# An S4D and SwiGLU layer on one core: an own DRAM tensor for the last spectra, other PSUM banks for the second FFN block, filler products, constant biases, and a new order table

## The chip, the cores and the metric

The kernel runs on one core of one Trainium2 chip. The metric is device time in microseconds (us) of one execution. Before the change three runs gave 954.37, 955.36 and 956.51, median 955.36. The trace is of one further, profiled execution of 954.89 us, whose span from the first to the last instruction is 953.1 us.

The engines are TensorE (PE: matrix products), VectorE (DVE), ScalarE (ACT), GpSimd (POOL) and SyncE (SP, which here only issues DMA transfers).

## The reference

Input `A_u` is 2048 positions of D = 640 channels in f32. A layer norm with modulation feeds an S4D convolution (a kernel of 2048 taps per channel, made from 128 complex modes, applied by FFT); its result, gated, is added. A second layer norm with modulation feeds a SwiGLU network with F = 1728, which is gated and added too.

```python
mod = (_silu(c) @ w_mod).reshape(c.shape[0], 6, 1, -1)
h = _layernorm(x) * (1 + ca) + sa
P = jnp.exp((A * dt[:, None])[:, :, None] * pos[None, None, :])
K = 2.0 * jnp.einsum("dn,dnl->dl", C, P).real
y = jnp.fft.irfft(jnp.fft.rfft(u_t, L2) * jnp.fft.rfft(K, L2)[None], L2)[:, :, :L]
x = x + ga * (y + h * D_skip)
h = _layernorm(x) * (1 + cb) + sb
x = x + gb * ((_silu(h @ w1) * (h @ w3)) @ w2)
```

## The kernel before, in words

**Convolution stage, 0 to about 355 us.** The 640 channels are five blocks of 128, each of eight chunks of 16 channels: 40 chunks, named by their first channel (`ph_0`, `ph_16`, ...). One chunk of the convolution's kernel is made by `gen_chunk`: POOL adds phases (`ph`) and multiplies magnitudes (`yy`, `xx`), ACT takes sines and cosines (`tr`), DVE multiplies them (`yy`, `xx`; the last multiplication is `xx<-tr,xx`), and PE forms the chunk's taps as 64 small products into `kps`, whose copy `ks` ACT takes away. The cosine is ACT's sine with a bias of half pi; that bias stands in a tile `hpi`. Around the chunks lie the modulation row (`pm`, `prow`, `rw`, `wb`), the first layer norm (ACT sums and squares `xs`, DVE statistics `h_st`, `h_mv`, a square root by Newton steps `rs_..._h`, normalised rows `hn`, `hb`) and the spectra: `ps`, `fh`, `fk` are products on the way to the frequency side, `fz` the last ones before the inverse, copied to `zt` and stored to DRAM as `zd`.

**Transition, about 355 to 430 us.** The inverse products `iy` read rows of `zd` back (`iz`, `xb`, `izb`). Channels 0 to 511 of the first eight row groups (two blocks of 512 positions, 0 and 1) come first (`iy0` to `iy7`); then the last 128 channels, whose spectra are made last, are stored and loaded back by `last_load` (tiles `izb0`, `izb1`, four transfers each, on SP's queue) for the products `iyb0` and `iyb1`. DVE adds them to the residual (`x`, `late`) and takes statistics (`st`, `mv`) and the Newton steps (`rs_..._n`); ACT and DVE normalise (`xn`); PE transposes (`tp`); ACT shifts (`v`) and splits into a high part (`x0h`, ...), DVE makes the low part (`x0l`, ...). The index in `x0`, `x1`, `x7`, `x4`, ... is only that of a buffer. The weights of the first FFN tiles are split likewise (`wh_u`, `wl_u`).

**FFN, about 376 us to the end.** The 1728 columns are 14 tiles (tile 13 is half), the positions four blocks of 512. Products with high and low parts (`hh`, `lh`, `hl`: three for one) give gate and up in `gu` banks. Tiles 0 and 13 come first for blocks 0 and 1: the steps `pp0.0` to `pp0.4` for block 0, `pp1.0` to `pp1.4` for block 1, each a fifth of the depth. The transposes `tp` of block 1 stand between them. Tile 1 follows as `pq0`, `pq1`, with the down products `dn0`, `dn13`, `dn1` between them, which add into five accumulator banks (`acc0` to `acc4`). From about 430 us on, groups of products for the other tiles and blocks run (`X`, `c`, `acc`); blocks 2 and 3 load their rows `iz8` to `iz15` by `inverse_row`.

**What sets the order.** Up to the first FFN group the kernel is a list of some 1690 tasks with what each needs. The text `ORDER` lists their numbers; `Plan.sequence` goes through it and checks that needs and buffers are met; `Plan.run` then issues each task, so each engine executes its tasks in this order and waits at a task whose inputs are not there. [...]

## Time and profile before

| stretch | what runs | us |
|---|---|---|
| profiled execution | one run | 954.89 |
| its span | first to last instruction | 953.1 |
| mean granted PE clock | whole span | 0.979 |
| PE busy | whole span | 870.5 |
| DVE busy | whole span | 682.3 |
| ACT busy | whole span | 551.5 |
| POOL busy | whole span, nearly all of it up to 320 us | 344.1 |

A row of the timeline gives the start, the duration, the engine, the line, the operation, output and inputs, the number of instructions that were joined in the row, and in brackets the idle time before it with what ended it. A granted clock of 1.00 is full speed of PE, 0.5 half. In the page's slices the busy share of the four computing engines and PE's clock, in tenths, lie like this over the span (40 slices of 23.8 us):

```profile
PE   1266999999989997899999999999999999999997
DVE  7988999999989878776676775657555555555412
ACT  3989999998877733644444444545444444443312
POOL 2698999999987400011111111000121212120000
PEclk9987999999999997999999999999999999999999
```

PE has little to do in the first four slices, while DVE, ACT and POOL are busy; slices 15 and 16 (357 to 405 us) are the transition.

### The profile page before, as it was taken

The page shows a single profiled execution, that of the slowest core. Times are in us where ns is not written, and L with a number is a line of the kernel's source. Part 1 is how long each engine was busy: PE and PEld are TensorE (multiplying, and loading weights), DVE is VectorE, ACT ScalarE, POOL GpSimd, SP SyncE. Part 2 cuts the span into 40 slices and gives each one's busy share as a digit, 9 for nine tenths or more (in the row PEclk, how much of TensorE's full clock was granted, in tenths as well). Part 3 has the DMA queues.
Part 4 walks back from the last instruction along what each step waited for, and adds up shares of the span by engine and source line. Part 5 has one row for each costly group of instructions (what it writes and reads, how often), then busy time and mean ns, then how long its engine had stood idle before and what let it go on. Part 6 is the DMA issues. An engine that isn't in the chain of part 4 may idle for free.

```text
span 953.1 us, 21244 instructions
## 1 busy us (share of the span) xinstructions
PE 870.5 (91%) x8369; PEld 689.6 (72%) x8369; DVE 682.3 (72%) x1290; ACT 551.5 (58%) x1036; POOL 344.1 (36%) x376
## 2 busy tenths in 40 slices
PE   1266999999989997899999999999999999999997
PEld 1134968877878875686777778888788888888775
DVE  7988999999989878776676775657555555555412
ACT  3989999998877733644444444545444444443312
POOL 2698999999987400011111111000121212120000
PEclk9987999999999997999999999999999999999999
DMA  9974454453173578754444412375432222221374
GB/s 199 284 266 112 158 134 137 101 146 83 47 173 93 134 189 212 179 179 125 148 116 123 139 63 91 92 237 168 130 91 84 83 84 83 84 84 38 110 217 132
DMA packets 110508, 127.42 MB, mean 134 GB/s; under 512 B 10568, under 2 KB 90696, under 8 KB 109128
## 3 DMA queue, kind: packets, MB, share of 16 engines
q1 hardware_dynamic: 110120, 125.80, 46.9%
q8 instruction: 66, 1.08, 0.5%
q14 instruction: 34, 0.28, 0.1%
q10 hardware_dynamic: 288, 0.26, 0.1%
HBM read 95.89 MB, written 30.15 MB: 132 GB/s over the span
## 4 chain that ended last, share of the span: by engine, by line
PE 55%; DMA 2%; ACT 2%; DVE 2%; SPq 1%; issue 1%; DVEq 0%
PE c L150 19%; PE acc L150 18%; PE X L150 12%; PE gu L150 3%; PE iy L150 1%; DMA w2r<-in_w 1%; DMA w<-w2d 1%; PE to L150 1%; PE tp L150 1%; PE gh L150 1%; ACT oc L978 0%; PE iyb L150 0%; SPq L991 0%; DMA izb<-zd 0%; DMA zd<-zt 0%
## 5 line engine op out<-in xcount | busy, mean ns | idle before, releaser
L150 PE MATMUL acc<-ah,w 128*128 128x512 f32 x560 | 173.0, 394 | 3.0 <-DMA w<-w2d 2.3
L150 PEld LDWEIGHTS acc<-ah,w 128*128 128x128 f32 x560 | 103.7, 188 | 26.6 <-issue 2.7
L775 POOL TENSOR_TENSOR s<-wr 128x256 f32<-128x256 f32 x22 | 16.6, 753 | 277.3 <-DMA wr<-in_w 133.0
L150 PE MATMUL acc<-al,w 128*128 128x512 f32 x260 | 102.2, 393 | 0.0
L599 DVE TENSOR_TENSOR wl<-s,wh 128x256 fp32r<-128x256 f32 x92 | 39.0, 424 | 67.3 <-ACT wh L598 66.8
L598 ACT ACTIVATE wh<-s 128x256 fp32r<-128x256 f32 x92 | 37.6, 410 | 78.3 <-PE X L150 57.9
L150 POOL TENSOR_TENSOR ph<-p,p 128x1024 int32<-128x1024 int32 x40 | 79.0, 1974 | 6.4 <-ACT tr L150 4.2
L598 ACT ACTIVATE wh<-wr 128x256 fp32r<-128x256 f32 x92 | 38.4, 418 | 57.6 <-PE X L150 42.0
L776 POOL TENSOR_TENSOR s<-s,wr 128x256 f32<-128x256 f32 x22 | 16.6, 753 | 132.2 <-issue 130.9
L150 DVE TENSOR_TENSOR yy<-yy,tr 128x512 f32<-128x512 f32 (+1 forms) x60 | 56.8, 947 | 6.3 <-POOL yy L150 3.3
L150 PE MATMUL kps<-yy,xx 128*32 128x64 f32 x1920 | 38.2, 230 | 22.4 <-DVE xx L150 19.9
L150 ACT ACTIVATE tr<-ph,hpi 128x512 f32<-128x512 f32 x80 | 54.4, 689 | 6.9 <-DVE yy L150 5.9
L836 ACT ACTIVATE t<-g 128x512 f32<-128x512 f32 x44 | 27.8, 632 | 52.7 <-DVE g L800 52.7
L150 PEld LDWEIGHTS acc<-al,w 128*128 128x128 f32 x260 | 48.9, 188 | 10.8 <-DVE al L599 0.4
L805 DVE SCALAR_TENSOR_TENSOR g<-t,g 128x512 f32<-128x512 f32 x48 | 33.7, 702 | 31.2 <-ACT t L836 29.3
L150 PEld LDWEIGHTS kps<-yy,xx 128*32 128x32 f32 x1920 | 32.7, 114 | 31.1 <-issue 17.5
L150 DVE TENSOR_TENSOR xx<-tr,xx 128x512 f32<-128x512 f32 x80 | 54.3, 683 | 0.7
L150 PE MATMUL fz<-fp,wz 64*128 64x512 f32 x224 | 54.5, 607 | 0.1
L599 DVE TENSOR_TENSOR wl<-wr,wh 128x256 fp32r<-128x256 f32 x92 | 40.7, 443 | 14.8 <-ACT wh L598 14.7
L150 ACT ACTIVATE tr<-ph 128x512 f32<-128x512 int32 x80 | 46.5, 598 | 4.2 <-DVE yy L150 2.7
L150 PE MATMUL ps<-wk,xb 128*64 128x128 f32 x640 | 46.8, 294 | 1.2 <-DVE hb L150 0.4
L598 ACT ACTIVATE ah<-h 128x512 fp32r<-128x512 f32 x26 | 16.5, 633 | 53.8 <-PE acc L150 53.8
(452 smaller groups left out, 2450.7 us busy)
## 6 DMA issues: line engine op xcount, KB each, us to landing
w<-w2d SPq DMA_DIRECT2D x42, 640.0 KB, 3.9
wr<-in_w SPq DMA_DIRECT2D x50, 320.0 KB, 3.6
zd<-zt SPq DMA_DIRECT2D x40, 256.0 KB, 2.5
w2d<-w SPq DMA_DIRECT2D x14, 640.0 KB, 3.5
xs<-in_x SPq DMA_DIRECT2D x16, 320.0 KB, 10.9
hs<-hb SPq DMA_DIRECT2D x20, 256.0 KB, 2.8
xb<-hs SPq DMA_DIRECT2D x20, 256.0 KB, 5.5
iz<-zd SPq DMA_DIRECT2D x32, 160.0 KB, 4.3
```

The source lines that it names most:

```text
L150: self.prev = self.k.order(f(*a, **kw), self.prev)
L598: self.nc.scalar.activation(H, v, AF.Copy)
L599: eng.tensor_tensor(Lo, v, H.bitcast(F32), op=ALU.subtract)
L775: eng.tensor_tensor(s[0], u[:, 0:2], u[:, 2:4], op=ALU.add)
L776: eng.tensor_tensor(s[1], s[0], g[:, 0:2], op=ALU.subtract)
L805: V.scalar_tensor_tensor(g, th, 1.0, g, op0=ALU.add, op1=ALU.mult)
L836: tanh = lambda o, i: A.activation(o, i, AF.Tanh, scale=0.5)
```

## The change

1. **`hpi` goes.** The bias of the cosines is the constant `HPI`.
2. **DRAM tensor `zl`.** The last block's spectra are stored there, `zd` keeps the other 512 channels. `last_load` reads block b's part with two transfers of 256 KB rather than four of 128 KB, one on SP's queue and one on ACT's. `inverse_row` needs eight transfers instead of four a row.
3. **Statistics.** The second layer norm takes a row's statistics in two instructions (512 and 128 columns) rather than five of 128; they are combined from 12 numbers instead of 30.
4. **Bank `small`.** One PSUM tile of 512 columns has the tag `kg` for good. `kps` is its columns 256 to 511; the first norm's sums, squares and statistics (`h_sum`, `h_ss`, `h_mv`) and two temporaries of the modulation are in its first columns.
5. **Fillers.** `wa0`, `wb0` to `wb4`, `wc0` and `wc1` are tasks of four 128x128 products of the identity with itself whose results nobody reads: `wa0` behind `iy7`, `wb0` before `iyb0`, the other `wb` between `iyb0` and `iyb1`, `wc` within `pq0`.
6. **Second block's first tiles.** `pp1` writes accumulator banks (`own=True`), so it takes no `gu` banks from `pp0`; `dn0`, which starts the accumulators, waits for `pp1`'s gates (`gm1.0`, `gm1.13`).
7. **`ORDER`** is a new list, and `Plan.sequence` counts buffers in use rather than asking for the oldest.

The core of the diff (the 1690 numbers of `ORDER` are left out):

```diff
+        self.small = psg.tile([P, 512], F32, name="small", tag="kg", bufs=1)
-                kps[c] = self.psg.tile([P, 256], F32, name=f"kps{b}{c}", tag="kg", bufs=1)
+                kps[c] = self.small[:, 256:]
-        for x in ("h_nm", "h_ss"):
-            setattr(self, x, self.gp.tile([P, NJ], F32, name=x))
+        self.h_nm = self.gp.tile([P, NJ], F32, name="h_nm")
+        self.h_sum, self.h_ss = self.small[:, 16:32], self.small[:, 32:48]
...
-                A.activation(t, ab[:, :, 4 - i, :], AF.Sin, scale=-SINS, bias=self.hpi)
+                A.activation(t, ab[:, :, 4 - i, :], AF.Sin, scale=-SINS, bias=HPI)
...
-        self.zd = d.tile([32, 2, 64, D], F32, name="zd")
+        self.zd = d.tile([32, 2, 64, D - P], F32, name="zd")
+        self.zl = d.tile([32, 2, 64, P], F32, name="zl")
...
-            for h in range(2):
-                for pr in range(2):
-                    t0 = 16 * (2 * pr + h) + 4 * b
-                    self.nc.sync.dma_start(z["b", b][h * 64:h * 64 + 64, pr], zv[:, t0:t0 + 4, cut:])
+            zl = self.zl.rearrange("f r (pr h t j) d -> (f r) h t pr (j d)", pr=2, h=2, t=4)
+            for h, e in enumerate((self.nc.sync, self.nc.scalar)):
+                e.dma_start(t[h * 64:h * 64 + 64].rearrange("p (r x) -> p r x", r=2), zl[:, h, b])
...
-                self.nc.sync.dma_start(z[pr][g * 64:(g + 1) * 64], zv[:, 16 * (2 * pr + g) + j])
+                for v, o in ((zv, slice(0, D - P)), (zl, slice(D - P, D))):
+                    self.nc.sync.dma_start(z[pr][g * 64:(g + 1) * 64, o], v[:, 16 * (2 * pr + g) + j, :o.stop - o.start])
...
-    def ln_part(self, st, xs, j, c0, c1):
-        for c in range(c0, c1):
-            self.nc.vector.bn_stats(st[:, j, c, :], xs[:, j, c * P:(c + 1) * P])
+    def ln_part(self, st, xs, j, c):
+        self.nc.vector.bn_stats(st[:, j, c, :], xs[:, j, 512 * c:min(512 * c + 512, D)])
...
+        def idle(n, place):
+            t = place()
+            for i in range(4):
+                nc.tensor.matmul(t[:, (i & 1) * P:(i & 1) * P + P], self.ident, self.ident, start=True, stop=True)
...
-                        banks[m] = [self.bank(f"gu{b}{m}{i}") for i in range(2 if m < 13 else 1)]
+                        banks[m] = [self.acc_bank(f"gu{b}{m}{i}", i if m < 13 else 2) if own else self.bank(f"gu{b}{m}{i}") for i in range(2 if m < 13 else 1)]
...
-        plain(1, (0, 13), "pp1.", 33, [])
+        plain(1, (0, 13), "pp1.", 33, [f"v1.{k}" for k in range(3)], True)
```

Three places show what the new order moves. The first is DVE's queue around chunk 0, whose last multiplication is the second `xx<-tr_0,xx`. Before:

```order
L150 SCALAR_TENSOR_TENSOR yy_315<-yy_315,tr_0_338 128x16x32
L150 BN_STATS h_st_235<-xs_230 128x6 x2
L150 COPY mag<-ptp 128x512
L150 BN_STATS h_st_235<-xs_230 128x6 x2
L150 TENSOR_TENSOR yy_315<-yy_315,tr_0_379 128x1024
L150 TENSOR_TENSOR xx_314<-tr_0_363,xx_314 128x512
L150 BN_STATS h_st_235<-xs_230 128x6 x2
L150 TENSOR_TENSOR xx_314<-tr_0_382,xx_314 128x512
```

In the changed kernel, on DVE around the same multiplication (`xx_272` is chunk 0, `xx_296` and `yy_297` chunk 1):

```order
L150 TENSOR_TENSOR xx_272<-tr_0_305,xx_272 128x512
L150 SCALAR_TENSOR_TENSOR small<-small,ct 128x5
L150 TENSOR_SCALAR sc<-small 128x5
L150 TENSOR_TENSOR xx_296<-tr_16_357,xx_296 128x512
L150 TENSOR_SCALAR h_nm<-small 128x4
L150 TENSOR_TENSOR xx_272<-tr_0_361,xx_272 128x512
L150 TENSOR_SCALAR pB<-ptp 128x4x128
L150 BN_STATS h_st_264<-xs_259 128x6 x2
L150 TENSOR_TENSOR yy_297<-yy_297,tr_16_338 128x16x32
L150 SCALAR_TENSOR_TENSOR yy_297<-yy_297,tr_16_338 128x16x32
```

The statistics `h_st` have moved behind chunk 0; before them stand small operations and one multiplication of chunk 1.

The second place is DVE's queue ahead of the add of `iyb0`, which starts the second norm of block 0. Before (the last rows of it):

```order
L150 TENSOR_TENSOR x_94<-iy_5338,x_94 128x512
L150 BN_STATS st_5020<-x_94 128x6 x2
L150 TENSOR_TENSOR late<-iy_5344,late 128x512
L150 BN_STATS st_5020<-x_94 128x6 x4
L150 TENSOR_TENSOR late<-iy_5357,late 128x512
L150 TENSOR_TENSOR late<-iy_5361,late 128x512
L150 BN_STATS st_5020<-x_94 128x6 x4
L150 TENSOR_TENSOR x_94<-iyb_5395,x_94 128x4x128
```

In the changed kernel, on DVE ahead of the same add (`st_4969` is block 1's, `st_4967` block 0's):

```order
L150 TENSOR_TENSOR late<-iy_5317,late 128x512
L150 TENSOR_TENSOR late<-iy_5321,late 128x512
L150 BN_STATS st_4969<-late 128x6
L150 TENSOR_TENSOR wl_u_5155<-wr_13_5041,wh_u_5154 128x128
L150 BN_STATS st_4969<-late 128x6
L150 TENSOR_TENSOR wl_u_5135<-wr_13_5041,wh_u_5134 128x256
L150 BN_STATS st_4967<-x_94 128x6 x2
L150 TENSOR_TENSOR x_94<-iyb_5362,x_94 128x4x128
```

Each statistics instruction now covers 512 columns, and two weight splits and block 1's statistics stand ahead of the add, which had come after it.

The third place is PE's queue at the second block's transposes and first products (`xn` are the normalised rows of block 1, `x4h`, `x4l` the first split operand of it, `gu_5679` and `gu_5618`, `gu_5620` the banks of `pp1`). Before, the end of the transposes and the start of `pp1`:

```order
L150 MATMUL tp_5664<-ident,xn_5623 128x128
L150 MATMUL tp_5664<-ident,xn_5606 128x128
L150 MATMUL tp_5664<-ident,xn_5604 128x128
L150 MATMUL tp_5664<-ident,xn_5617 128x128
L150 MATMUL gu_5679<-x4h_5669,wh_u_5065 128x512
L150 MATMUL gu_5679<-x4l_5670,wh_u_5065 128x512
```

In the changed kernel, on PE behind `pp1`'s first nine products:

```order
L150 MATMUL gu_5620<-x4h_5570,wl_u_5132 128x512
L150 MATMUL tp_5636<-ident,xn_5554 128x128
L150 MATMUL tp_5636<-ident,xn_5543 128x128
L150 MATMUL tp_5636<-ident,xn_5541 128x128
L150 MATMUL tp_5636<-ident,xn_5552 128x128
L150 MATMUL gu_5618<-x4h_5570,wh_u_5244 128x512
L150 MATMUL gu_5618<-x4l_5571,wh_u_5244 128x512
```

Before, all 20 transposes come first and `pp1` after them; now the transposes are put four by four between the steps of `pp0` and `pp1`, two of the five groups behind products of `pp1`.

More of the change, by code (lines that the diff above doesn't have):

```diff
@@ L228, in setup @@
         make_identity(nc, self.ident)
-        self.hpi = c.tile([P, 1], F32, name="hpi")
-        nc.gpsimd.memset(self.hpi, HPI)
         self.ones = c.tile([P, 1], F32, name="ones")
@@ L353, in h_stats @@
             st = self.gp.tile([P, 4, 2, 6], F32, name=f"h_st{b}", tag="h_st", bufs=1)
-            mv = self.gp.tile([P, 4, 2], F32, name=f"h_mv{b}", tag="h_mv", bufs=1)
+            mv = self.small[:, 64 + 8 * b:72 + 8 * b].rearrange("p (j a) -> p j a", a=2)
         def both(j):
@@ L1137, in tail_tasks @@
         ends = [f"z{b4}.{j}.o{f}" for j in range(4) for f in range(2)]
-        add("border", None, 0, border, ends + [f"ia{j}" for j in range(8)] + ["change"] + [f"wl0.{i}" for i in range(5)], 0)
+        add("border", None, 0, border, [f"wa{i}" for i in range(1)] + ends + [f"ia{j}" for j in range(8)] + ["change"] + [f"wl0.{i}" for i in range(5)], 0)
         def last_load(b):
@@ L1178, in mean @@
                 ln[b], steps[0] = self.ln_steps(self.fp, self.stats[b][1], f"n{b}")
-            add(f"lm{b}", "DVE", .68, mean, [f"isb{b}"] + [f"is{j}.{c}" for j in range(4 * b, 4 * b + 4) for c in range(2)], rank)
+            add(f"lm{b}", "DVE", .68, mean, [f"isb{b}"] + [f"is{j}" for j in range(4 * b, 4 * b + 4)], rank)
             if b == 0:
@@ L1230, in plain @@
                 need = [f"wl{m}.{i}" for m in tiles for i in ((k // 2,) if m == 13 else (4,) if k == 4 else (k // 2, 2 + k // 2))]
[L1231 removed]
+                add(p + f"{k}", "PE", .684 * len(take), lambda k=k: mm(k), [f"xl{b}.{k}"] + need + ([p + f"{k - 1}"] if k else after), rank, take=take if k == 0 and not own else [])
             last = [p + f"{KT - 1}"]
```

139 lines of the change are left out of this document (72 added, 67 removed), and 42 rows, old and new, of the table ORDER.

## The prediction

> **What bounds the kernel now.** The page names TensorE (PE) as the busiest engine, 91% of the span. Its idle rest is found with the view that cuts the span into stretches (columns: stretch, its length, PE busy, products, granted clock, DMA share, GB/s):
>
> ```profile
> core 0: us, PE busy (x), PEclk, DMA share, GB/s
> 0.00:50.70 50.70, 10.08 (x41) 0.95 0.94 251
> 50.70:80.00 29.30, 15.97 (x313) 0.79 0.59 192
> 80.00:100.00 20.00, 17.94 (x405) 0.91 0.67 169
> 100.00:355.00 255.00, 249.05 (x5044) 0.99 0.48 123
> 355.00:376.00 21.00, 15.40 (x83) 0.78 0.88 221
> 376.00:406.00 30.00, 26.45 (x116) 0.92 0.74 177
> 406.00:431.00 25.00, 23.84 (x105) 1.00 0.53 180
> 431.00:953.10 522.10, 511.74 (x2284) 1.00 0.38 115
> ```
>
> From 431 on PE works 511.74 of 522.1 us on instructions that the change leaves in order, so I cost that part at 0. From 100 to 355 it is busy 249.05 of 255, and F, the end of the last spectrum, lies where PE's work plus its idle time before puts it. That idle time is 100 − 10.08 − 15.97 − 17.94 = 56.0 us before 100, and 6 after. The view of waits up to 360 says for whom, and the timeline shows two of these waits:
>
> ```profile
> PE ptp L150 <- DVE wb L150: 25.1, 3, 9.4
> PE kps L150 <- DVE xx L150: 21.1, 6, 10.3
> ...
> 50.75 1.96 PE L150 MATMUL kps<-yy,xx 128*32 128x64 f32 x64 [7.65 <-DVE xx L150]
> 78.93 1.96 PE L150 MATMUL kps<-yy,xx 128*32 128x64 f32 x64 [10.35 <-DVE xx L150]
> ```
>
> So the early stage is worth what VectorE (DVE) brings forward for chunks 0 to 8. Behind F come the transition's waits, from the same view for 360 to 440:
>
> ```profile
> PE gu L150 <- ACT x4h L150: 2.1, 1, 2.1
> PE tp L150 <- ACT xn L150: 1.8, 1, 1.8
> PE iyb L150 <- DMA izb<-zd: 1.5, 2, 1.1
> PE c L150 <- DVE h L150: 1.2, 1, 1.2
> PE tp L150 <- DVE xn L150: 0.7, 1, 0.7
> PE gu L150 <- DVE x4l L150: 0.7, 1, 0.7
> ```
>
> **Term 1, the early order.** Ahead of chunk 0's last DVE product stand these two groups, as the view of groups by line and shape counts them (busy us, mean ns of one):
>
> ```profile
> L150 DVE BATCH_NORM_STATS2 h_st<-xs 128x6 f32<-128x320 f32 x8 | 3.5, 475 | 0.0
> ...
> L150 DVE COPY mag<-ptp 128x512 f32<-128x512 f32 x1 | 0.7, 670 | 0.0
> ```
>
> The new order puts all eight statistics and this copy behind it, 4.2 us. I add up every DVE instruction ahead of a chunk's last one in each program, at the durations of the rows before. The difference is −5.1 us at chunk 0, −8.4 at 1, −4.5 at 2, −3.9 at 3, between −1.8 and −5.2 at 4 to 9, −7.8 at 39, the last. For POOL it is +0.9, −4.5, +0.3, +2.6, +6.5 and +5.5 at chunks 0 to 5 and between −2 and +4.3 from 6 on. ACT gains through the constant:
>
> ```profile
> L150 ACT ACTIVATE tr<-ph,hpi 128x512 f32<-128x512 f32 x80 | 54.4, 689 | 6.9 <-DVE yy L150 5.9 <-DVE xx L150 0.3
> ...
> L150 ACT ACTIVATE tr<-ph 128x512 f32<-128x512 int32 x80 | 46.5, 598 | 4.2 <-DVE yy L150 2.7 <-POOL ph L150 0.7 <-DVE xx L150 0.5
> ```
>
> The 80 cosines read a bias from SBUF and take 689 ns, the 80 sines without it 598. If the bias is the reason, 80 × 0.091 = 7.3 us go from ACT; its moved work adds 3.4 up to the last chunk. Neither is on the path directly, since PE is the bound from 100 on.
>
> PE's own work to its last chunk is the same in both, so F moves by the idle time before 100, and that by the lead with which chunks 6 to 8, the last before PE is dense, come: −2.2 to −3.2. I take **−3**. The ends: −7, near the last chunk's lead, if each lead is kept; +3, if the bank described under the second rival eats the lead.
>
> **Term 2, the last spectra's way through DRAM and the first normalisation.** F is the end of the first row of the timeline here; behind it stand three groups:
>
> ```profile
> 350.04 4.67 PE L150 MATMUL fz<-fp,wz 64*128 64x512 f32 x16
> ...
> 358.99 5.21 SPq L150 DMA_DIRECT2D izb<-zd  x8
> ...
> 365.23 0.69 DVE L150 TENSOR_TENSOR x<-iyb,x 128x512 f32<-128x512 f32 x1 [1.00 <-PE iyb L150]
> ...
> 371.91 4.53 PE L150 MATMUL tp<-ident,xn 128*128 128x128 f32 x20 [1.80 <-ACT xn L150]
> ...
> 387.88 2.40 PE L150 MATMUL tp<-ident,xn 128*128 128x128 f32 x20 [0.74 <-DVE xn L150]
> ...
> L150 DVE BATCH_NORM_STATS2 st<-late 128x6 f32<-128x128 f32 x20 | 4.3, 279 | 0.0
> ...
> L150 DVE BATCH_NORM_AGGREGATE mv<-st 128x2 f32<-128x30 f32 x8 | 1.4, 245 | 0.0
> ...
> L150 DVE BATCH_NORM_AGGREGATE h_mv<-h_st 128x2 f32<-128x12 f32 x4 | 0.4, 160 | 0.0
> ```
>
> F = 354.71. Eight load issues, 0.65 us each, make SyncE send izb1's last at 364.2; four on two queues end 1.3 us after they begin, so block 0's landing comes about 1 us and block 1's about 3 us earlier. That doesn't bring the add of 365.23 forward: DVE now stands ahead of it. Between the last zt copy (end 0.74 after F, 355.45) and that add it has 8 adds of about 0.66 (5.3), 7 statistics of 512 columns and two weight splits (0.7). No row shows 512 columns; back to back one of 128 takes 4.3/20 = 0.22 and one of 320 3.5/8 = 0.44, and a straight line gives 0.65, so 4.55 in all; the bounds are 0.44 and 0.86, four of 128. The add starts at 366.0, **+0.8** (by the bounds −0.7 to +2.3). Four aggregates of 12 numbers instead of 30 give 4 × (1.4/8 − 0.4/4) = 0.3 back. tp starts **0.5 later** against F.
>
> Fillers: wb1 to wb4 are 16 products of 0.12 (2.40/20), 1.9 us, in a wait of PE's, so they cost 0. They end with iyb1 near 366.5, and some 5.5 us of idle PE remain until tp at 372.4. The stretch 355 to 376 has a mean clock of 0.78 and the 20 tp products there took 4.53, against 2.40 in the second block. I take tp at half clock again, 0; the other end is 4.53 − 2.40, −2.1.
>
> [...]
>
> **Term 3, first to third FFN tile.** One stretch, from the first gu product to the first X, and rows inside it:
>
> ```profile
> 376.09:428.27 52.18, 48.63 (x212) 0.96 0.66 181
> ...
> 386.35 0.91 ACT L150 ACTIVATE xn<-late,rs_n_n,rs_y_n 128x640 f32<-128x640 f32 x1
> ...
> 390.92 0.78 ACT L150 ACTIVATE v<-tp,cols 128x512 f32<-128x512 f32 x1
> ...
> 399.50 0.62 ACT L150 ACTIVATE x8h<-v 128x512 fp32r<-128x512 f32 x1
> ...
> 403.32 0.39 PE L150 MATMUL gu<-x8h,wh_u 128*128 128x512 f32 x1
> ...
> 405.15 0.39 PE L150 MATMUL gu<-x8h,wl_u 128*128 128x512 f32 x1
> ```
>
> It lasts 52.2 us. By the order it holds 190 products and tp1's 20 (two more reach over its edges). At (405.15 − 403.32)/8 = 0.229 and with tp1's 2.40 they make 45.9; 6.3 is waits and half clock. Now tp1 lies between pp0's and pp1's steps, pp1 has its own banks, and block 1's ACT normalisation isn't queued behind a weight copy (the 386.35 row, now some 4 us earlier). So the waits on xn and x4h (0.7 + 2.1 + 0.7) go and the half clock behind them with it. What comes: wc0 and wc1, 8 × 0.12 = 1.0; the start at half clock, 0.6; and a wait that is late next, on x5 and x8 of block 1, which stand behind gate work and tile 1's weight splits on ACT and DVE. In the old order ACT took 9 us from the first v (390.92) to x8h's end, a little more than pp0's and pp1's steps that now cover it, so I bound this wait by 0 and 5 and take 2.2, near the old one of 2.1 + 0.7. Sum: −6.3 + 1.0 + 0.6 + 2.2 = **−2.5**. With +0.5 the transition is −2.0 (from −5 to +1). The 1.2 us on DVE h I leave.
>
> **No cost.** Row loads iz8 to iz15 take 64 issues instead of 32, on SyncE, early against PE in a part where DMA is 0.38 busy; uncovered, 4 more issues of 0.65 a row delay an inverse row by 2.6 us, which PE passes by other products. The rsqrt's extra temporary costs 0.
>
> Sum against the profiled execution, 954.89: −3 − 2 = 949.9. It lies 0.47 below the median of the three runs, so the forecast for the median is **950.4**.
>
> **Rivals.**
> *Only the transition gains* (chance 0.15): POOL, with +2.1 to +6.5 of work ahead at chunks 3 to 7, and not DVE, releases the chunks; F stays: 953.4. For it speaks that POOL, too, has little idle time there; against it, that the waits name DVE xx.
> *Slower through the shared bank* (0.15): chunk products, ACT's sums and squares and DVE's aggregates now write the one bank `small`. In the new program chunk 0's product waits for a square, the next square for that product's end, chunk 1's product for an eviction queued behind another square, and DVE's aggregate for chunk 1's product.
>
> ```profile
> L150 ACT ACTIVATE ks<-kps 128x256 f32<-128x256 f32 x40 | 15.0, 375 | 4.9 <-PE kps L150 4.7
> L150 ACT ACTIVATE xs<-xs,h_nm 128x640 f32<-128x640 f32 x12 | 9.8, 813 | 0.5 <-DVE h_nm L150 0.5
> ```
>
> One round is a cold product (1.96, the 50.75 row), a square (0.81) and an eviction (0.38), 3.2 us; three rounds are at most 10. It decides once more than chunk 3's lead of 3.9 is lost. Half of the excess of 6 is F + 3; with 1 us less of the transition's gain, since ACT then also enters it later, 957.
>
> [...]
>
> *All is kept* (0.17): leads of 6 us in F, and no late x5, x8: −6 − 5 = 944.
> *The fillers and the pair of queues do nothing* (0.08): tp is cold in any case, DVE sets the add, and x5 and x8 eat term 3: 952.4.
>
> **Numbers.** Forecast (947 to 953 at the median) 0.45; the four rivals 0.15, 0.15, 0.17, 0.08. A difference within 0.2%, 1.9 us, can't be told from none. The first rival lies at that border, half of it counts as same; with a share of the forecast's upper edge: faster 0.72, same 0.13, slower 0.15. The range leaves out the outer halves of the extremes: 943.5 to 957.
>
> **What would show it.** Right: first kps product near 46, chunk 3's near 75, F near 351.7; cosine rows near 600 ns; the iyb0 add about 11.3 us after F, ended by DVE's queue and not by izb; tp still 4.5 us; gu to X in 49.7 us. Wrong: PE waiting on ACT squares or DVE aggregates before 70, F later than 355, or a wait of over 4 us on x5, x8 or weights of tile 1.

## The result: 979.3 us after, 955.0 before

Four runs of the changed kernel have a median of 979.34 us (976.82 to 981.41), four of the kernel before beside them 954.95 (954.37 to 956.51). The ratio is 1.0252, with a 95% interval of 1.0223 to 1.0280: the change makes the kernel slower by 24 us. The forecast was 950.4, in a range of 943.5 to 957.

The profiled execution of the changed kernel took 978.61 us, its span is 976.8 (953.1 before). Split at the prediction's marks (F is the end of the last spectrum, X the first product into a bank `X`, with which the third FFN tile begins), the 23.7 us by which the span grew lie for the most part in two of three parts, ahead of F and behind X:

| | before | after | difference |
|---|---|---|---|
| start to F | 354.71 | 367.56 | +12.85 |
| F to first transpose tp | 17.20 | 16.57 | −0.63 |
| F to first gu product | 21.38 | 19.46 | −1.92 |
| F to X | 73.56 | 75.74 | +2.18 |
| X to the end (the tail) | 524.83 | 533.50 | +8.67 |

### The profile page after: what moved, and what is told of

Its sections match the earlier page's. It is cut to its first block, busy times and chain, and to the rows that moved or that the text cites. A ratio compares the mean times of both kernels' runs of the same rounds, so it can differ in the third digit from the quotient of the medians.

```text
span 976.8 us, 21320 instructions
## 1 busy us (share of the span) xinstructions
PE 885.8 (91%) x8433; PEld 694.7 (71%) x8433; DVE 675.0 (69%) x1235; ACT 549.4 (56%) x1043; POOL 350.1 (36%) x375
## 4 chain that ended last, share of the span: by engine, by line
PE 72%; DVE 10%; ACT 7%; issue 3%; DMA 2%; SPq 1%; DVEq 0%; ACTq 0%
PE c L150 19%; PE acc L150 17%; PE X L150 12%; PE ps L150 6%; PE small L150 4%; PE fz L150 4%; PE fh L150 3%; PE fk L150 3%; DVE fp L150 1%; PE iy L150 1%; PE gu L150 1%; DMA w2r<-in_w 1%; DVE yy L150 1%; DVE xx L150 1%; ACT tr L150 1%
## 5 line engine op out<-in xcount | busy, mean ns | idle before, releaser
L150 PE MATMUL acc<-ah,w 128*128 128x512 f32 x560 | 175.3, 398 | 1.7 <-DMA w<-w2d 1.2
L150 ACT ACTIVATE tr<-ph 128x512 f32<-128x512 f32 (+1 forms) x160 | 93.6, 600 | 7.9 <-DVE yy L150 4.0
L775 POOL TENSOR_TENSOR s<-wr 128x256 f32<-128x256 f32 x22 | 17.4, 791 | 176.6 <-DVE wl L597 86.5
L150 PE MATMUL ps<-wk,ks 128*64 128x128 f32 x640 | 42.9, 286 | 14.6 <-DVE hb L150 8.6
L777 POOL TENSOR_TENSOR s<-wr 128x256 f32<-128x256 f32 x22 | 18.8, 853 | 96.9 <-ACT wh L150 65.2
L150 PEld LDWEIGHTS ps<-wk,ks 128*64 128x64 f32 x640 | 37.1, 143 | 20.4 <-issue 12.9
```

Of the source, the lines that this page charges most:

```text
L150: self.prev = self.k.order(f(*a, **kw), self.prev)
L775: eng.tensor_tensor(s[0], u[:, 0:2], u[:, 2:4], op=ALU.add)
L777: eng.tensor_tensor(s[2], g[:, 0:2], u[:, 0:2], op=ALU.subtract)
```

## The profile after

The view of stretches, cut at the same events (stretch, its length, PE busy, products, granted clock, DMA share, GB/s):

```profile
core 0: us, PE busy (x), PEclk, DMA share, GB/s
0.00:50.70 50.70, 9.28 (x53) 1.00 0.92 227
50.70:80.00 29.30, 16.10 (x272) 0.78 0.53 153
80.00:100.00 20.00, 16.02 (x330) 0.84 0.86 227
100.00:367.60 267.60, 252.99 (x5148) 0.99 0.47 123
367.60:387.00 19.40, 18.23 (x132) 1.00 0.91 212
387.00:418.00 31.00, 26.01 (x120) 1.00 0.62 178
418.00:443.30 25.30, 25.30 (x111) 0.93 0.36 102
443.30:976.80 533.50, 521.87 (x2291) 1.00 0.38 116
```

Three things are to be seen. Between 100 and F PE was idle for 6 us before; now it is for 267.60 − 252.99 = 14.6. Behind F the clock is 1.00 where it was 0.78. And in the last row PE is as busy as before, at full clock, but busy for 521.87 us where the tail before had 513.3: the same products take longer.

Of PE's waits on `DVE xx` in the first 100 us, 20.5 us before, the view of waits has 1.3 left; others have taken their place, and PE is idle for 58.6 us before 100 where it was 56.0:

```profile
PE ptp L150 <- DVE wb L150: 30.6, 3, 15.1
PE ps L150 <- DVE hb L150: 8.6, 1, 8.6
```

The timeline of all engines between 50 and 67, cut to the bank `small`, shows the round of rival two:

```profile
50.21 1.95 PE L150 MATMUL small<-yy,xx 128*32 128x64 f32 x64
...
52.58 0.83 ACT L150 ACTIVATE xs<-xs,h_nm 128x640 f32<-128x640 f32 x1 [1.99 <-PE small L150]
55.32 0.39 ACT L150 ACTIVATE ks<-small 128x256 f32<-128x256 f32 x1
...
57.70 0.83 ACT L150 ACTIVATE xs<-xs,h_nm 128x640 f32<-128x640 f32 x1 [1.50 <-PE small L150]
62.17 0.97 DVE L150 BATCH_NORM_AGGREGATE small<-h_st 128x2 f32<-128x12 f32 x4 [3.79 <-ACT xs L150]
...
63.64 0.83 ACT L150 ACTIVATE xs<-xs,h_nm 128x640 f32<-128x640 f32 x1 [1.02 <-DVE small L150]
```

ACT's squares wait for chunk products, DVE's aggregate waits for ACT's squares, the next square for the aggregate: 8.3 us of such waits in 12 us (1.99, 1.50, 3.79 and 1.02), of operations that share no number and only a bank. Whether operations that share a bank need such waits, no run here shows. They are waits of ACT and DVE, not of PE; what they cost F, the experiments show.

The cosines, in the view of groups by line and shape (busy us, mean ns of one):

```profile
L150 ACT ACTIVATE tr<-ph 128x512 f32<-128x512 f32 x80 | 47.1, 599 | 4.6 <-DVE xx L150 2.1 <-DVE yy L150 1.6
```

They take 599 ns instead of 689, as forecast. DVE's timeline behind F, cut to the last statistics ahead of the add of `iyb0`:

```profile
377.38 1.28 DVE L150 BATCH_NORM_STATS2 st<-x 128x6 f32<-128x512 f32 x2
378.58 0.67 DVE L150 TENSOR_TENSOR x<-iyb,x 128x512 f32<-128x512 f32 x1
```

The add starts 11.0 us after F and waits for nothing but the instructions ahead of it. The transition on PE, first the second norm and then the places with fillers and waits:

```profile
374.51 1.16 PE L150 MATMUL small<-ident 128*128 128x128 f32 x8
375.73 1.16 PE L150 MATMUL wb<-ident 128*128 128x128 f32 x8
...
377.84 4.81 PE L150 MATMUL wb<-ident 128*128 128x128 f32 x32
...
384.13 0.33 PE L150 MATMUL tp<-ident,xn 128*128 128x128 f32 x1 [0.46 <-ACT xn L150]
384.94 2.29 PE L150 MATMUL tp<-ident,xn 128*128 128x128 f32 x19 [0.48 <-ACT xn L150]
...
408.75 0.50 PE L150 MATMUL gu<-x5l,wh_u 128*128 128x512 f32 x1 [1.06 <-DVE x5l L150]
411.39 0.50 PE L150 MATMUL gu<-x8l,wh_u 128*128 128x512 f32 x1 [0.23 <-DVE x8l L150]
417.93 1.52 PE L150 MATMUL wc<-ident 128*128 128x128 f32 x8 [3.01 <-DVE h L150]
424.67 1.05 PE L150 MATMUL wc<-ident 128*128 128x128 f32 x8
...
447.02 0.50 PE L150 MATMUL c<-x1h,wh 128*128 128x512 f32 x1 [2.16 <-DVE h L150]
```

A filler task of four products shows as eight in the records and takes 1.16 to 1.2 us ahead of tp. With these fillers the clock is 1.00 from 367.6 to 387.0 (no_wb, below, is the kernel without them), and the transposes take 2.6 us; before, they took 4.53 us, at a granted clock of 0.50 from 371.9 to 376.1. `wc0` waits 3.01 us, since the accumulator bank that it writes still holds `pp1`'s gates.

## The experiments

Where the table gives no interval, one run was made, and a single run says little about 3 us: eight runs of one kernel below lie between 949.75 and 958.47. F and the other marks come from one profile of each kernel, F as the end of its last `fz` row, and repeat better. Five kernels share the changed kernel's program up to F but for addresses or fillers, and their F lies between 366.8 and 369.6; three share that of the kernel before but for addresses (before, before_st512, before_wp0), and theirs lies between 354.3 and 355.6.

| kernel | time, us | ratio to before (95%) | F | chunk 30 | F to X | tail | spacing |
|---|---|---|---|---|---|---|---|
| before | 954.95 | | 354.71 | 266.3 | 73.56 | 524.83 | 0.2291 |
| after | 979.34 | 1.0252 [1.0223, 1.0280] | 367.56 | 278.5 | 75.74 | 533.50 | 0.2333 |
| st_old | 971.96 | 1.0155 [1.0102, 1.0208] | 368.06 | 279.6 | 75.39 | 528.25 | 0.2291 |
| before_st512 | 964.67 | 1.0094 [1.0055, 1.0133] | 355.58 | 267.2 | 75.29 | 532.73 | 0.2333 |
| pad24 | 968.74 | | 366.76 | 277.6 | 75.14 | 525.10 | 0.2273 |
| before_wp0 | 965.17 | 1.0115 [1.0033, 1.0196] | 354.32 | 265.9 | 77.08 | 532.90 | 0.2333 |
| order_old | 970.19 | 1.0137 [1.0099, 1.0175] | 356.99 | 268.8 | 78.66 | 532.85 | 0.2333 |
| small_split | 977.63 | 1.0214 [1.0174, 1.0254] | 363.00 | 274.4 | 75.70 | 536.60 | 0.2333 |
| old_split | 968.08 | | 352.81 | 265.6 | 80.87 | 532.62 | 0.2333 |
| before_hpi | 954.53 | 0.9990 [0.9955, 1.0026] | 351.69 | 266.2 | 74.91 | 527.00 | 0.2291 |
| mid_split | 976.76 | | 358.97 | 273.5 | 77.32 | 538.71 | 0.2333 |
| strict | 1015.81 | 1.0622 [1.0572, 1.0673] | 404.60 | 316.0 | 76.87 | 535.33 | 0.2333 |
| strict_split | 1014.02 | | 399.66 | 311.0 | 76.98 | 535.56 | 0.2333 |
| bank_split | 976.05 | | 362.02 | 275.7 | 76.88 | 535.30 | 0.2333 |
| knot30 | 978.88 | 1.0240 [1.0184, 1.0295] | 366.54 | 270.5 | 75.73 | 535.63 | 0.2333 |
| no_wc | 977.42 | | 369.58 | 280.4 | 69.66 | 536.36 | 0.2333 |
| no_wb | 982.37 | | 368.06 | 278.2 | 76.09 | 536.45 | 0.2333 |
| best1 | 956.94 | | 352.83 | 265.9 | 71.15 | 531.22 | 0.2291 |
| best3 | 998.15 | 1.0433 [1.0383, 1.0484] | 398.37 | 309.7 | 69.33 | 530.20 | 0.2292 |

Chunk 30 is the start of the small product that closes it. Spacing is the mean distance, in us, from the start of one 512-column product to the start of the next in the tail, over the some 2,000 pairs of each trace that start 0.21 to 0.25 us apart.

### The tail: where the FFN's weights lie

The first theory on the tail was an address: the third part of the change makes the tile `ln_st` smaller, and the FFN's tiles behind it move. By the allocations in the built programs, the activations of the FFN's products then start at 32 modulo 128 bytes of a partition instead of 96, and their weights at 96 instead of 32. st_old gives the tile its old size back and uses a part of it:

```diff
-        return (pool.tile([P, 4, 2, 6], F32, name=f"st_{tag}", tag="ln_st", bufs=2),
+        return (pool.tile([P, 4, KT, 6], F32, name=f"st_{tag}", tag="ln_st", bufs=2)[:, :, :2, :],
```

> The changed kernel with the statistics tile of the second norm kept at its old size of 480 bytes (only 192 are used), so that every FFN operand lies at the SBUF address, modulo 128, that it had before the change (moving operand 96, weights 32; in the changed kernel 32 and 96). Address theory: the 512-column products of the FFN return from one every 0.2333 us to one every 0.2287, some 2200 of them, so the time falls by about 10 us to 969; the conv stage stays as it is (last spectrum's end near 367.6). Rival theory, the slower spacing comes from something else in the changed program (the order of the PSUM banks, other transfers beside it): the spacing stays 0.233 and the time 979.

before_st512 does the opposite to the kernel before, and nothing else:

```diff
-        return (pool.tile([P, 4, KT, 6], F32, name=f"st_{tag}", tag="ln_st", bufs=2),
+        return (pool.tile([P, 4 * KT * 6 + 8], F32, name=f"st_{tag}", tag="ln_st", bufs=2)[:, :4 * KT * 6].rearrange("p (j c s) -> p j c s", j=4, c=KT),
```

> The kernel before with the statistics tile made 32 bytes larger, nothing else: FFN operands get the addresses modulo 128 of the changed kernel (32 and 96). Address theory: the spacing of FFN products rises from 0.2287 to 0.2333 us and the time from 955 to about 965. Rival theory, something else in the changed program: 955 and 0.2287.

Both move the spacing by the whole difference. The row of 800 to 900 in the view of stretches, where PE has almost no wait, shows it as products in 100 us, before and after:

```profile
800.00:900.00 100.00, 99.62 (x441) 1.00 0.23 73
```

```profile
800.00:900.00 100.00, 100.00 (x430) 1.00 0.24 73
```

There are 438 products in that row of st_old and 429 in that of before_st512, and the clock is 1.00 in all four. Eight floats of padding in the kernel before cost 8.1 us (964.67 against 956.57 beside it), the old tile size gives the changed kernel 7.4 back (979.34 to 971.96). Which operand's address matters, two paddings tell. In pad24 a constant tile of 40 floats becomes one of 24, so that of the two operands only the weights move, to 32; in before_wp0 a tile of 32 becomes 24, and the weights move to 0:

```diff
-        c.tile([P, 40], F32, name="pad")
+        c.tile([P, 24], F32, name="pad")
```

> The changed kernel with the constants' pad 64 bytes shorter: the FFN weights' addresses go from 96 back to 32 modulo 128, the moving operands stay at 32 (96 before). If the weights' address is what slows the products, the spacing returns to 0.229 us and the time to about 970; if it is the moving operands' address, the spacing stays at 0.233 and the time near 979.

> The kernel before with the constants' pad 32 bytes shorter: the FFN weights' address goes from 32 to 0 modulo 128, nothing else. With the weights at 32 the 512-column products come every 0.229 us, at 96 every 0.233. If the cost is that a weight row of 512 bytes begins late in a line of 128, 0 is as good as 32 or better: 0.229 or less, time 955 or up to 10 us less. If only 32 is good, 0 is slow too: 0.233 and 964.

| kernel | activations, mod 128 | weights, mod 128 | products from 800 to 900 | spacing, us |
|---|---|---|---|---|
| before | 96 | 32 | 441 | 0.2291 |
| st_old | 96 | 32 | 438 | 0.2291 |
| pad24 | 32 | 32 | 443 | 0.2273 |
| after | 32 | 96 | 430 | 0.2333 |
| before_st512 | 32 | 96 | 429 | 0.2333 |
| before_wp0 | 96 | 0 | 429 | 0.2333 |

In these six traces the weights' address decides between two groups: at 32 the products follow each other in 0.2273 to 0.2291 us, at 0 and 96 in 0.2333, with the activations at 96 as at 32. With the weights at 32, pad24 is a little faster still (0.2273 against 0.2291); whether that is its activations' address or another tile that moved with the padding, one kernel can't tell. 64 was not tried. The first theory for before_wp0, that the late start of a weight row costs the time, fails, since 0 is as slow as 96; why 32 is the fast one, no run here shows. The 0.0042 us on the tail's 2,106 products of 512 columns are 8.8 us, and PE's busy time in the tail went from 513.30 to 521.87, 8.57 more; so the tail's 8.67 are explained by it. Beside that, tails of one spacing differ from profile to profile, from 524.83 to 531.22 us at the fast one and from 532.62 to 538.71 at the slow one, and no run shows why.

### Up to F: bank and order

order_old is the changed kernel with the old order, task by task (new tasks beside their neighbours):

```diff
-ORDER = """(the new list)"""
+ORDER = """(the old list's order, in the new tasks' numbers)"""
```

> The changed kernel with the old order table, carried over task by task (the fillers put at the places that the new order gives them, a row's statistics where their second part stood). Order theory: the late end of the last spectrum comes from the new order; it returns from 367.6 to about 355 and the time falls by some 10 us to 967 to 970. Bank theory: the waits on the one PSUM bank for first-norm sums, squares and chunk products make the loss; then they appear in this order too (PE or ACT waiting on each other between 45 and 70 us), the last spectrum ends at 362 or later and the time stays above 972. Address theory is not touched: product spacing 0.2333.

small_split keeps the new order and puts sums, squares and statistics back into SBUF tiles; old_split does both:

```diff
-        self.h_sum, self.h_ss = self.small[:, 16:32], self.small[:, 32:48]
+        self.h_sum, self.h_ss = (self.gp.tile([P, NJ], F32, name=x) for x in ("h_sum", "h_ss"))
...
-        th, u = self.small[:, :KT], self.small[:, 8:8 + KT]
+        th, u = (e.tile([P, KT], F32, name=x) for x in ("th", "thu"))
...
-            mv = self.small[:, 64 + 8 * b:72 + 8 * b].rearrange("p (j a) -> p j a", a=2)
+            mv = self.gp.tile([P, 4, 2], F32, name=f"h_mv{b}", tag="h_mv", bufs=1)
```

> The changed kernel with the first norm's sums, squares, statistics and the modulation's temporaries back in SBUF tiles, so that only chunk products use the bank. Bank theory: ACT's waits of 2.0 and 1.5 us on PE, DVE's of 3.8 us on ACT and PE's on DVE between 50 and 66 us go, chunk 3 comes 3 to 5 us earlier, and the last spectrum's end falls from 367.6 by as much; the time is 972 to 976. Order theory: the waits go, but chunks 4 to 39 are held by the order, and the time stays within 2 us of 979. Product spacing stays 0.2333 in both.

> The changed kernel with both: the old order table, and the first norm's sums, squares and statistics in SBUF tiles. It closes a square of four: with the new order the last spectrum ends at 367.6 (shared bank) and 360.6 (SBUF tiles), with the old order at 357.0 (shared bank). If order and bank were independent, the two would add up and this kernel would end its last spectrum near 350.0. If the bank costs what the waits in the old order show, some 2 us, and the new order's 5.9 us are its own, it ends near 354.7, that of the kernel before, and the time is about 968.

F in the four kernels: 367.56 (new order, bank), 363.00 (new, SBUF), 356.99 (old, bank), 352.81 (old, SBUF). For small_split that is the end of its last `fz` row:

```profile
358.34 4.66 PE L150 MATMUL fz<-fp,wz 64*128 64x512 f32 x16
```

The expectations that name small_split's F give 360.6, a time at which these products still run, and what they work out from it is 2.4 us off. With 363.0 the sum of the two parts, had they nothing to do with each other, would be 352.4 for old_split, and 352.81 was measured: they add up. The bank costs 4.2 us of F with the old order and 4.6 with the new, and the order costs 10.2 us without the bank and 10.6 with it. The chunks (start of the product that closes each, and F) show where each loss comes in:

| chunk | before | old order, SBUF | new order, SBUF | new order, bank (after) |
|---|---|---|---|---|
| 1 | 62.0 | 62.0 | 58.3 | 57.3 |
| 3 | 80.8 | 80.8 | 79.4 | 83.9 |
| 6 | 99.1 | 98.9 | 97.7 | 102.0 |
| 7 | 105.0 | 104.4 | 107.1 | 111.4 |
| 29 | 261.2 | 260.4 | 261.4 | 265.6 |
| 30 | 266.3 | 265.6 | 274.4 | 278.5 |
| 39 | 328.9 | 327.1 | 336.1 | 340.7 |
| F | 354.71 | 352.81 | 363.00 | 367.56 |

The bank's loss is there by chunk 3 and passes unchanged to F, 4.1 to 4.6 us at each row of the table from chunk 3 on. It lies where the waits between 50 and 66 are. In the time it can't be told from noise: 979.34 and 977.63 have intervals that overlap, and of order_old and old_split (970.19 and 968.08) the second ran once. The order's cost is clear in the time too (979.34 against 970.19). What remains, 352.81 against 354.71, can be the constant, which before_hpi tries alone in the kernel before:

```diff
-                A.activation(t, ab[:, :, 4 - i, :], AF.Sin, scale=-SINS, bias=self.hpi)
+                A.activation(t, ab[:, :, 4 - i, :], AF.Sin, scale=-SINS, bias=HPI)
```

> The kernel before with the constant as the bias of the cosines, nothing else (the tile stays, so that no address moves). ACT's 80 cosines take 600 ns instead of 689, 7 us less ACT work in the conv stage. The old order with SBUF tiles and the other parts of the change ended its last spectrum 1.9 us earlier than the kernel before; if the constant is the cause, this one does too and the time is 953.5. If PE alone sets that end, no change: 955.4.

F falls by 3.0 there, and the time can't be told from none (0.9990, 0.9955 to 1.0026).

Where does the order lose its 10 us? The rows of old_split in the view of stretches, and those of small_split, with only the order between them:

```profile
0.00:100.00 100.00, 42.89 (x751) 0.95 0.80 223
100.00:250.00 150.00, 146.20 (x3038) 1.00 0.43 112
250.00:300.00 50.00, 47.58 (x1042) 1.00 0.43 105
300.00:352.80 52.80, 52.24 (x968) 1.00 0.66 163
```

```profile
0.00:100.00 100.00, 44.68 (x755) 0.95 0.77 206
100.00:250.00 150.00, 144.17 (x3032) 1.00 0.45 120
250.00:300.00 50.00, 42.27 (x884) 0.97 0.39 93
300.00:363.00 63.00, 61.20 (x1130) 1.00 0.62 163
```

Up to 100 the new order has 1.8 us less idle time on PE, and chunks 1 to 6 come earlier, the direction that the forecast had. Behind it, idle time grows by 2.0 us up to 250, by 5.3 between 250 and 300 and by 1.2 from there. Together that is 6.8 us; the other 3.4 are busy time, 292.3 instead of 288.9 us, for the same number of products of each kind, and no run shows what makes them. The timeline of small_split names the place, first PE, then POOL:

```profile
268.48 1.09 PE L150 MATMUL ps<-wk,ks 128*64 128x128 f32 x16 [2.43 <-DVE fp L150]
...
286.52 0.67 PE L150 MATMUL small<-yy,xx 128*32 128x64 f32 x26 [3.27 <-issue]
```

```profile
274.56 1.06 POOL L150 TENSOR_TENSOR yy<-e,e 128x512 f32<-128x512 f32 x1 [4.97 <-PE small L150]
```

PE stands for a bank that DVE's `fp` has yet to leave; chunk 30's product comes behind eleven other steps and at 274.4 instead of 265.6; POOL, which needs that chunk's buffer, stands for 4.97 us; and a later chunk's product then stands half done for 3.27.

mid_split takes the new order up to chunk 29's product and the old one from there on:

> The changed kernel with the first norm's sums in SBUF tiles (whose last spectrum ends at 360.6 with the new order and at 352.8 with the old one), and an order that is the new one up to chunk 29's product, the old one from there to the border, and the new one behind it. If the jam at chunk 30 (PE waits for DVE's fp, DVE for PE's ps, POOL 4.9 us for PE) is what the new order costs there, the last spectrum ends near 353. If the loss is spread over the whole order, near 358 to 360.

Chunk 30 is still at 273.5, and F at 358.97 is 4.0 earlier than small_split's and 6.2 later than old_split's. By these single profiles, the new list's arrangement of the last ten chunks is part of the loss and not all of it. The rest may be what the new order has left undone by chunk 29, which comes ahead of chunk 30 in either list; that is argued and not measured.

The next theory was the seventh part of the change. The relaxed rule lets a task take a buffer of a rotating set while the oldest holder is still in use, and the new list does so at 41 places, 38 of them up to the last spectrum (none in the old one), among them the `ps` step that waits 2.43. strict and strict_split hold each such task back until the oldest holder is done, bank_split does so for the PSUM banks only, best3 adds all other repairs:

> The changed kernel with its order repaired at 38 places: up to the border task a task takes the next buffer of a rotating set (bank, tr, zt, hz, xx, f2) only once the set's oldest holder is done in the order, as it always was before the change; up to 37 tasks at a time are held back for it, nothing else moves. Theory 1, PE stands behind such a buffer: the waits ps on ACT sp and DVE fp and fz on DVE fp between 150 and 275 (7.3 us together) go, chunk 30's product comes 5 to 8 us earlier than 278.5, F falls from 367.6 by 5 to 9 to 359 to 362, the time from 979 to 970 to 974. Theory 2, the order's loss is what stands ahead on POOL and DVE: F stays within 366 to 370, time 976 to 981. The tail keeps its slow spacing (0.233).

> The same repaired order, with sums, squares and aggregates back in SBUF tiles instead of the bank 'small' (to be held against the kernel with the SBUF tiles alone: F 360.6, chunk 30 at 274.4). Theory 1: chunk 30 at 266 to 269, F 352 to 355, time 966 to 970. Theory 2: F 359 to 362, time 974 to 979.

> As before it, but only the PSUM set 'bank' is repaired (8 places, up to 4 tasks held back), the SBUF sets stay as the new order has them. If the banks that PE's steps take are what matters: F as in the kernel with all six sets repaired, within 1.5. If the cosine and inverse tiles (tr, zt) matter: F stays at 359 to 361.

> Repaired order, SBUF tiles for sums and squares, ln_st at its old tile size (so weights at 32 mod 128 again) and the fillers wc0 and wc1 without products. If the three causes (buffers, bank, weights' address) and the late fillers are the whole loss: F 352 to 355, spacing 0.229, F to X 69 to 72, time 948 to 955, not slower than before. If the order costs something else: F over 358 and time 957 to 963.

None of these kernels supports this theory. bank_split's F is 362.02 against 363.00, less than profiles of one program differ by, and strict_split's 399.66, worse by 37 us; strict (404.60) and best3 (398.37) are as late. Much of strict_split's idle time is in the row of 150 to 200 and the next:

```profile
150.00:200.00 50.00, 37.11 (x750) 0.86 0.38 101
200.00:250.00 50.00, 38.46 (x642) 0.84 0.22 60
```

The tasks held back come late for those that follow, so these kernels don't measure what the relaxed rule costs in a list that was searched without it; that stays open.

knot30 moves only the eleven steps ahead of chunk 30 behind its product:

> The changed kernel with SBUF tiles for sums and squares (F 360.6) and one knot of its order undone: eleven steps (the PE steps k3.0 to k3.3 and hh3.0, hh3.1 with their evictions), which the new order puts between the chunks 29 and 30, stand behind chunk 30's product instead. Holding tasks back for the rotating sets has been shown to make it worse, so this theory is: these steps, each in a bank that DVE has yet to read, jam PE and DVE, POOL waits 4.97 us at 274.6 for PE, and chunk 31 is late for that. By it the waits ps on DVE fp (2.4), POOL's 4.97 and PE's 3.3 at 286.5 go, chunk 30 comes at 264 to 268 instead of 274.4, F at 355 to 357, time 971 to 974. Rival: the steps jam wherever they stand, or the next chunk is late instead; F 359 to 362, time 975 to 979. Of the 8.6 us of idle PE that the new order adds between 100 and F, 5.3 lie between 250 and 300, so F cannot fall by much more than 5.3 by this.

Chunk 30 comes 3.9 us earlier, at 270.5, but not by as much as expected, and two other waits take the place of those removed, as PE's timeline shows:

```profile
268.59 1.96 PE L151 MATMUL small<-yy,xx 128*32 128x64 f32 x64 [5.25 <-ACT tr L151]
...
289.52 0.67 PE L151 MATMUL small<-yy,xx 128*32 128x64 f32 x26 [3.76 <-issue]
```

Chunk 30's cosines themselves were late on ACT; chunk 31 is at 281.6 instead of 279.4, and F is 366.54, later by 3.5 than small_split's and than either theory had it. The rival's mechanism was right: the next thing is late. So it is shown that the order costs 10.2 to 10.6 us of F, and that 8.6 us more idle time of PE between 100 and F, 5.3 of it between 250 and 300, around chunk 30, are the larger part of that. Which of its rules makes it is not settled: PE, DVE, ACT and POOL are all late there, and no move of a few steps brought it back.

### The transition: fillers

no_wc and no_wb keep the tasks in their places and leave out their products, those of `wc`, and those of `wa` and `wb`:

```diff
-            add(f"wc{i}", "PE", .88, lambda i=i: idle(i, lambda: later(i)), ["v1.0"] + ([f"wc{i - 1}"] if i else []), 17)
+            add(f"wc{i}", "PE", .88, None, ["v1.0"] + ([f"wc{i - 1}"] if i else []), 17)
```

> The changed kernel without the eight products of the fillers wc0 and wc1 (the only thing left out). Filler theory: these products go to an accumulator bank that the second block's first tile still holds until DVE has read its gate, so PE waits 3.0 us in the midst of pq0 and then works 2.6 us for nothing; without them the first X product comes 5 to 6 us earlier after the last spectrum (75.7 becomes about 70) and the time is 973 to 975. Rival: the wait is only moved, to the next product that needs the same DVE results (dn0, which starts the accumulators, or the c products of 447 us); then at most the 2.6 us of work are saved and the time is 976 to 978.

> The changed kernel without the products of the fillers wa0 and wb0 to wb4 (the only thing left out); wc0 and wc1 stay. If the fillers keep PE's clock up, tp's 20 products take 4.5 us instead of 2.6 and the first gu product comes 1.5 to 2 us later after the last spectrum than 19.46. The block 1 add, whose iyb1 products stand behind wb4, comes some 5 us earlier. If the clock stays up without them, tp takes 2.6 and gu comes at 19.5 or a little earlier.

Without `wc`, X comes 6.1 us earlier against F. The wait of 3.0 and the products' 2.6 are most of that; the granted clock, too, had fallen behind that wait, to 0.79 between 417 and 425, and in no_wc it is 1.00 from the first gu product to X. So these fillers, far from keeping the clock up, came with a lower one. Of the 6.1 us, 1.2 are lost again at the next wait, which grows from 2.16, as PE's timeline of no_wc shows:

```profile
444.13 0.50 PE L150 MATMUL c<-x1h,wh 128*128 128x512 f32 x1 [3.33 <-DVE h L150]
```

From F to the end no_wc takes 606.0 us, the changed kernel 609.2, so half of it is left. The time of its single run, 977.42, is the rival's, though X came where the filler theory had it: F was 2.0 us later in that profile.

Without `wa` and `wb` a lower clock comes back, 0.75 from F to the first gu product, and the transposes take 4.1 us, as that stretch and PE's transposes in no_wb show:

```profile
368.06:388.78 20.72, 14.05 (x86) 0.75 0.92 207
...
384.62 0.47 PE L150 MATMUL tp<-ident,xn 128*128 128x128 f32 x1 [3.18 <-ACT xn L150]
385.43 3.59 PE L150 MATMUL tp<-ident,xn 128*128 128x128 f32 x19 [0.34 <-ACT xn L150]
```

The first gu product is 1.26 later against F and X 0.35: the cost is mostly hidden behind what waits next.

best1 is the best combination that was found: the old order up to the last spectrum and the new one behind, SBUF tiles, the old `ln_st`, no `wc` products, the constant.

> A kernel put together from the parts: the changed kernel with the old order up to the border and the new one behind it, the first norm's sums in SBUF tiles, the statistics tile at its old size, and without wc0 and wc1. Expected from the parts: last spectrum at 354.7, first X product 70 us behind it, and 526 to 528 from there to the end: 951 to 953, against 953.1 before. If the transition's new order doesn't fit the old order ahead of it (other transfers late), the first X product comes 74 us or more behind the last spectrum and the time is 956 or more.

Its single run took 956.94 us beside 955.13 of the kernel before, and F and the way to X are 1.9 and 2.4 us shorter than before. Of these 4.3 only 1.4 are left at the first `c` product (429.55 against 430.97), since it waits 4.03 us for DVE's `h` instead of 1.16: at that product, DVE sets the pace. Its tail is 6.4 us longer than that of the kernel before at the same spacing, 2.9 of it ahead of that product; the rest is open. No kernel of this study is shown to beat the kernel before.

## Why the prediction was wrong

**The tail at 0** ("PE works 511.74 of 522.1 us on instructions that the change leaves in order, so I cost that part at 0"). This step failed. The instructions are the same and in the same order, but PE's time for them was not (513.30 us before, 521.87 after): the weights' addresses moved with the size of a tile in part 3 (from 32 to 96 modulo 128), and the products' spacing by 1.8% (0.2291 to 0.2333). +8.67 us, for which neither a term nor a rival existed.

**Term 1, −3.** F went up by 12.85: 10.2 for the order, 4.6 for the bank, 1.9 back. Two steps failed. The first is that the work ahead of a chunk was added up for each engine by itself; waits from engine to engine were not. DVE's sum gave chunk 0 a lead of 5.1 us; its last multiplication started at 49.03 instead of 49.94, and its product at 50.21 instead of near 46, since DVE now waits for POOL and ACT for 3.8 us between 36 and 50, where it waited for 1.6. The longest of these waits and that multiplication in its timeline:

```profile
48.08 0.17 DVE L150 SCALAR_TENSOR_TENSOR small<-small,ct 128x5 f32<-128x5 f32 x1 [1.65 <-ACT xs L150]
...
49.03 0.68 DVE L150 TENSOR_TENSOR xx<-tr,xx 128x512 f32<-128x512 f32 x1
```

The bank is not the reason, for without it that multiplication starts at 49.37. The leads of chunks 6 to 8, taken as 2.2 to 3.2 us, were without the bank 1.2 at chunk 6, and chunks 7 and 8 came 2.7 and 0.7 later. The second step is that F moves by the idle time before 100, with the 6 us after it unchanged. From old_split to small_split the idle time before 100 falls by 1.8 us, so the direction was right there; but between 100 and F it rises by 8.6 us, where the prediction took "PE's own work is the same in both" as enough. The constant had its forecast size, 599 ns, and is worth some 2 to 3 us in F, where the prediction put it at nothing.

**Rival two, the bank (F + 3, chance 0.15).** Its mechanism and its place were right: a square waits for a product, the aggregate for a square, the next square for the aggregate, between 50 and 66. One wait was named wrongly: the aggregate stood behind a square and not behind chunk 1's product. Its size was near: it set the bank at 6 us against the forecast (F at +3 instead of −3), and taking it away gives 4.2 and 4.6. What failed is its chance, and the hope that it would be the only loss up to F.

**Term 2, +0.5.** The add of `iyb0` started 11.0 us after F (forecast 11.3), behind DVE's queue and not `izb`, and a statistics instruction of 512 columns took 0.64 back to back (forecast 0.65). But tp started 0.63 us earlier against F, not 0.5 later: from the add to it pass 5.55 us instead of 6.68, and only 0.3 of that was forecast. Wrong was also the half clock: `wb1` to `wb4` were taken as 1.9 us and took 4.81, because one of their products takes 0.30 us, not 0.12, and `wb0` and `wa0`, 1.16 each, were not counted. With them the clock from F to the first gu product is 1.00 (0.75 in no_wb, without them), and from tp to gu pass 2.89 us instead of 4.18: 1.3 of the 2.1 that the prediction had as the other end. So gu starts 1.92 earlier. The rows between 367.6 and 384.9 have no idle time of a microsecond, and a clock of 1.00; after how much idle time the clock falls, no run here shows.

**Term 3, −2.5.** Measured 56.28 − 52.18 = +4.1. The old waits on xn and x4h are gone, and x5 and x8 cost 1.06 + 0.23 = 1.3 instead of 2.2. The term mis-sized is the fillers `wc`: 1.0 was forecast, for the products; they cost 2.6 and 3.0 of waiting for the bank that they write. Without them the stretch is 50.22, 2.0 shorter than before. The wider spacing is in it too, an estimate of 0.8 us for its 190 products (0.0042 each).

**No cost** for the smaller row loads held: the view of waits shows no inverse row waiting for them.

## What to carry to other kernels

Before a stretch that PE fills is costed at nothing, compare the addresses of its operands in both programs, not only its instructions; a changed tile size far from the loop cost it 1.8% here (0.2291 to 0.2333 us a product). Work ahead of an instruction, added up for each engine, had the direction of the first chunks here and not the size, since an engine with less work ahead began to wait for others (DVE for 3.8 us between 36 and 50, where it was 1.6); and it says nothing on the idle time that a new order makes later: look for the steps that stand closer behind what releases them. Look at what holds a filler's bank: `wc0` waited 3.01 us for its own here, and without the `wc` products X came 6.1 us earlier against F.

## What the runs showed of the hardware that was not expected

- In the six kernels before, after, st_old, before_st512, pad24 and before_wp0, TensorE's 512-column products follow each other in 0.2273 to 0.2291 us where the weights lie at 32 modulo 128 bytes (441, 438 and 443 products from 800 to 900 in before, st_old and pad24) and in 0.2333 where they lie at 0 or 96 (430, 429 and 429 in after, before_st512 and before_wp0), at a granted clock of 1.00 there. The 0.2333 was measured with the activations at 32 (after, before_st512) and at 96 (before_wp0).
- A product of the identity with itself, 128x128 in f32, counts as two in the records and takes 1.16/4 = 0.29 us in `wa0` and `wb0` of the changed kernel and 4.81/16 = 0.30 in `wb1` to `wb4`, at a clock of 1.00, while 20 transposes of the same size take 2.40 us in the kernel before (the row of 387.88, clock 1.00), 0.12 each.
